# Gated mix of full and dilated local attention on one core: result products of two score sets together, bounds as sign-masked query rows, two head groups in the same rows

## The chip, the cores and the metric

The kernel runs on one core of a Trainium2 chip. The metric is the device time of one execution in microseconds (us). The kernel before has a median of 978.01 us over three runs (965.67, 978.01 and 978.8 us). The profile is of one execution, whose span from the first to the last instruction is 971.8 us.

## The reference

The input x is 2048 rows of 512 bf16 values. Two attention blocks with 32 heads of 16 values each run on the same x and are mixed by a gate per row:

```python
g = sigmoid((x * gate_w).sum(-1, keepdims=True))
# A: full attention
scores = einsum("bhqd,bhkd->bhqk", q, k) * (Dh ** -0.5)
a = (softmax(scores) @ v) @ A_wo
# B: 8 keys per row, at distances 0, 2, ..., 14; rows before the first are masked
b = (local dilated attention of x with B_wqkv) @ B_wo
out = g * a + (1 - g) * b
```

Here q, k and v are x @ wqkv, cut into heads. B_x isn't used.

## The kernel before, in words

**Block A.** The queries come in 4 chunks of 512 and the heads in 8 groups of 4. One chunk and one group make a *period*; there are 32. In a period, the unit of work is a *block*: one head's scores of 128 keys against 512 queries, 64 blocks to a period. PE makes the scores (q_proj and k_proj give `qt` and `kt_all`; each head fills 32 rows, 16 of values, one of a bound and 15 of zeros), four heads in four row groups of the array. ScalarE takes the exponential out of PSUM into a bf16 tile `pT`. PE multiplies that by the values `vp_all`, whose 17th column is 1 and so gives the softmax's denominator, into the one PSUM bank `acc`, four heads in four column groups.

Blocks go through PSUM in *sets* of alternately 3 and 2 (rings rA and rB, one buffer each); one activation covers a set. `pT` has two buffers per ring. The exponential needs no exact row maximum: a bound on each score is subtracted, sum of |q| times the largest |k|. For that, q_proj writes qt with a shift of 175 in the bound row, takes the absolute values (`absq`), multiplies them on PE by `selk_all` (minus the largest |k| in a column for the bound row) and adds the product to qt.

**VectorE blocks.** The last blocks of a period (`n_dve` of them, 129 in all) have their exponential made by VectorE in place of ScalarE, from a score in PSUM tag `misc`: step `dt` (linear, fp32), two steps `dg` and one `pd`, which build the bf16 bits. The three steps after dt take two blocks at once if there are two. Their values are scaled by 2^-56 in `vd_all`, a copy of the last two key tiles of vp_all.

**End of a period.** VectorE transposes acc in 32x32 squares (`accT`), divides by the denominator (`rden`, `ott`), and transposes back into `oat`. A head group of 4 heads fills 64 of the 128 rows of one slice of oat, eight slices per chunk, and the output product uses `woarr`, whose unused rows are zero.

**Block B** goes in 16 tiles of 128 rows, spaced 46.7 us in the plan. PE projects, VectorE evicts (`kvs`, `qb`), SP stores keys and values to DRAM and loads them back shifted (`ksh`, `vsh`). GpSimd multiplies and adds (`prod`, logits `lg`), VectorE and ScalarE do the small softmax (`mx`, `lg`, `ssum`, `rr`), GpSimd applies it to the values (`ob`, `obb`), PE transposes (`obt`).

**Order.** Each step is an Op with an engine, a duration in the planner's mind, what it needs, the buffers that it takes, and a due time. list_schedule (line 76) makes of them one fixed order per engine, in which each engine then runs (chain_on, line 180). An engine that waits for one step holds up all behind it. Where the result products of the last 3.2 us of the plan are few, the planner adds a *filler* in front of a result product: four matmuls that add zeros to acc (`acc<-ones_t,z`, line 789 on), to keep PE busy.

**Lines that matter here.** mm_heads 215, init 286 to 308, loads 318 to 356, k_proj 399, selk 423, v_proj 442, q_proj 482, b_tile 573, result products pv_mm 744 and the set loop 760 to 805, VectorE blocks d_group 809, end of a period 874 to 900, output products 906 to 980. In the profile, all operations of VectorE, ScalarE, GpSimd and SP that go through the chain have line 200, all matmuls line 209; the tiles tell them apart.

Of the kernel before, what the change touches and what calls it, by code (L numbers as in the profile page):

```python
# [18 lines left out]
    n_dve=(2,) * 4 + (3,) * 4 + (4,) * 17 + (6,) * 6 + (5,),  # L19
    dve_tiles=2,  # L20
    b_start=32.0,
# [13 lines left out]
SHIFT = 175.0  # L35
DEXP = 56
FRAC = 65536.0
# [18 lines left out]
class Op:  # L56

    def __init__(self, eng, occ, fn, dl, deps=(), alloc=(), use=(), lat=None, rel=0.0, name="",
                 dense=0, fill=False, after=()):
        self.eng, self.occ, self.fn, self.dl, self.rel, self.name = eng, occ, fn, dl, rel, name  # L60
        self.dense, self.fill, self.filled = dense, fill, False
        self.after = [d for d in after if d is not None]
        self.deps, self.alloc = [d for d in deps if d is not None], list(alloc)
        self.lat = (occ if not callable(occ) else occ(0.0)) + LAT[eng] if lat is None else lat
        self.done = None
        for tk in list(alloc) + list(use):
            tk.ops.append(self)
# [4 lines left out]
WAVE = lambda n: 0.2 + 0.22 * n  # L72
# [3 lines left out]
def list_schedule(ops):  # L76
# [28 lines left out]
    out, recent = [], []  # L105
    while len(out) < len(ops):
# [15 lines left out]
        lat = o.lat  # L122
        if o.dense:
# [19 lines left out]
def kernel(  # L143
# [71 lines left out]
    def mm_heads(out, c, col, rhs, start, stop):  # L215
        for j in range(4):
            mm(out[32 * j:32 * j + 32, :], wst[:, c, col + j * DH:col + j * DH + 32], rhs, start, stop, tile_position=(0, 32 * j))
# [16 lines left out]
    UNIT = 0.457  # L234
    T0 = 22.0
# [23 lines left out]
    wst = const.tile([128, DC, 3 * D], BF16, name="wst")  # L259
# [6 lines left out]
    woarr = const.tile([128, NG, D], BF16, name="woarr")  # L266
# [3 lines left out]
    rowc = const.tile([128, 3], FP32, name="rowc")  # L270
    z32 = const.tile([128, 32], BF16, name="z32")
    selq = const.tile([128, 128], BF16, name="selq")
# [3 lines left out]
    vd_all = const.tile([128, NTD, H, DH + 1], BF16, name="vd_all")  # L276
    kmax_all = const.tile([128, NG, NC], FP32, name="kmax_all")
    kmax = const.tile([128, NG], FP32, name="kmax")
    selk_all = const.tile([128, NG, 128], BF16, name="selk_all")
# [6 lines left out]
    def init_dve():  # L286
        V.memset(ones_t[:], 1.0)
        V.memset(selq[:], 0.0)
        V.memset(rowc[:], 0.0)
        for j in range(4):  # L290
            V.memset(selq[32 * j:32 * j + DH, 32 * j + DH:32 * j + DH + 1], 1.0)
            V.memset(rowc[32 * j:32 * j + DH + 1, 1:2], 1.0)
            V.memset(rowc[32 * j:32 * j + DH + 1, 2:3], SHIFT)
            V.memset(rowc[32 * j:32 * j + DH, 0:1], 1.0)
            V.memset(rowc[32 * j:32 * j + DH, 1:3], 0.0)
# [6 lines left out]
    def init_pool2():  # L302
        make_identity(nc, identf[:])
        G.memset(vp_all[:, 0, :, :], 1.0)
        G.memset(vp_all[:, 1:NT, :, DH:DH + 1], 1.0)

    def init_pool3():
        G.memset(woarr[:], 0.0)
# [4 lines left out]
    o_wz = op("pool", 3.6, init_pool3, -7.0, deps=[o_init_p])  # L313
# [4 lines left out]
    def load_x(sc):  # L318
        def s():
            if sc < 2:  # L320
                xl = work.tile([128, W, D], BF16, name="xld", tag="ksh", bufs=2)
            else:
                xl = work.tile([128, NG, QW], BF16, name="xld2", tag="oat", bufs=2)
# [3 lines left out]

    def load_w(part):
        def s():
            SP.dma_start(out=wst[:, :, part * D:(part + 1) * D], in_=a_w3[:, :, part * D:(part + 1) * D])  # L330
# [7 lines left out]
    def load_wo():  # L338
        SP.dma_start(out=bwo[:], in_=B_wo.rearrange("(c p) n -> p c n", p=128))
        wo4 = A_wo.rearrange("(i j d) n -> j d i n", j=4, d=DH)  # L340
        for j in range(4):
            SP.dma_start(out=woarr[32 * j:32 * j + DH, :, :], in_=wo4[j])
        SP.dma_start(out=kv_scr[0:16, 0:D], in_=woarr[16:32, 0, :])
        SP.dma_start(out=kv_scr[0:16, D:2 * D], in_=woarr[16:32, 1, :])
# [4 lines left out]
    o_wk = op("sp", 0.5, load_w(1), -8.9, lat=6.5)  # L349
    o_x[1] = op("sp", 0.5, load_x(1), -8.8, alloc=[xtok[1]], lat=7.5)  # L350
    o_x[2] = op("sp", 0.5, load_x(2), -8.7, alloc=[xtok[2]], lat=9.5)
    o_wq = op("sp", 0.5, load_w(0), -8.6, lat=11.0)
    o_x[3] = op("sp", 0.5, load_x(3), -8.5, alloc=[xtok[3]], lat=12.0)
    o_wv = op("sp", 0.5, load_w(2), -8.4, lat=13.0)
    o_bw = op("sp", 1.0, load_bw, -8.3, lat=19.0)
    o_wo = op("sp", 3.5, load_wo, -8.2, deps=[o_wz], lat=24.0)


    def warm():
        t_ = misc_ps([128, QW])  # L360
        for _ in range(3):
            mm_ct(t_, selq[:], ones_t[:], True, True)
# [36 lines left out]
    def k_proj(i, sc, tag, dl, rel=0.0):  # L399
# [3 lines left out]
        def part(c0, c1):  # L403
            def s():
                if c0 == 0:
                    st["pk"] = misc_ps([128, QW], tag=tag)
                for c in range(c0, c1):
                    mm_heads(st["pk"], c, D + 4 * i * DH, xT[:, c, sc * QW:(sc + 1) * QW], c == 0, c == DC - 1)
# [6 lines left out]
        def km():  # L415
            V.tensor_reduce(out=kmax_all[:, i, sc:sc + 1], in_=kt_all[:, i, sc * QW:(sc + 1) * QW],
                            axis=AX.X, op=ALU.max, apply_absolute_value=True)
        a = op("pe", WAVE(2), part(0, 2), dl - 2.6, dense=8, deps=[o_wk, o_init_d] + o_xt[sc], alloc=[tk], rel=rel, name=f"kp{i}.{sc}")
        b = op("pe", WAVE(2), part(2, DC), dl - 2.0, dense=8, deps=[a], use=[tk])
        c = op("dve", 0.71, kc, dl - 0.8, deps=[b], use=[tk])  # L420
        return op("dve", 0.70, km, dl, deps=[c])

    def selk(i, dl):
        def s():
            V.tensor_reduce(out=kmax[:, i:i + 1], in_=kmax_all[:, i, :], axis=AX.X, op=ALU.max)
            V.tensor_scalar(out=selk_all[:, i, :], in0=selq[:], scalar1=kmax[:, i:i + 1], scalar2=-1.0,
                            op0=ALU.mult, op1=ALU.mult)
        o_selk[i] = op("dve", 0.55, s, dl, deps=o_kc[i])
# [13 lines left out]
    def v_proj(h0, h1, tb, TB, tag, dl, rel=0.0):  # L442
# [4 lines left out]
        def mk(half):  # L447
            def s():
                if half == 0:
                    st["pv"] = misc_ps([128, TB, n], tag=tag)  # L450
                for tt in range(half * TB // 2, (half + 1) * TB // 2):
                    t = tb + tt
                    for c in range(DC):
                        mm(st["pv"][:, tt, :], xT[:, c, t * 128:(t + 1) * 128],
                           wst[:, c, 2 * D + h0 * DH:2 * D + h1 * DH], c == 0, c == DC - 1)
            return s

        def ev():
            V.tensor_copy(out=vp_all[:, tb:tb + TB, h0:h1, 0:DH], in_=st["pv"][:].rearrange("p t (h d) -> p t h d", d=DH))
            for t in range(max(tb, NT - NTD), tb + TB):  # L460
                V.tensor_scalar(out=vd_all[:, t - (NT - NTD), h0:h1, :], in0=vp_all[:, t, h0:h1, :],
                                scalar1=2.0 ** -DEXP, scalar2=None, op0=ALU.mult)
        xs = [o for sc in range(NC) if sc * TPC < tb + TB and (sc + 1) * TPC > tb for o in o_xt[sc]]
        a = op("pe", 0.62, mk(0), dl - 2.0, dense=8, deps=[o_wv] + xs, alloc=[tk], rel=rel, name=f"vp{h0}.{tb}")
        b = op("pe", 0.62, mk(1), dl - 1.4, dense=8, deps=[a], use=[tk])
        c = op("dve", 0.72 + 0.27 * max(0, tb + TB - (NT - NTD)), ev, dl, deps=[b, o_init_p], use=[tk])
# [15 lines left out]
    def q_proj(pi, tag, dl, rel=0.0):  # L482
# [4 lines left out]
        ta = tok("absq", 1)  # L487
        q_tok[pi] = tq

        def part(c0, c1):  # L490
            def s():
                if c0 == 0:
                    st["p1"] = misc_ps([128, QW], tag=tag)
                    st["absq"] = work.tile([128, QW], BF16, name="absq", tag="absq", bufs=1)
                    qt_tiles[pi] = work.tile([128, QW], BF16, name="qt", tag="qt", bufs=3)
                for c in range(c0, c1):
                    mm_heads(st["p1"], c, 4 * i * DH, xT[:, c, c_ * QW:(c_ + 1) * QW], c == 0, c == DC - 1)
            return s

        def ab():  # L500
            V.tensor_scalar(out=qt_tiles[pi][:], in0=st["p1"][:], scalar1=rowc[:, 0:1], scalar2=rowc[:, 2:3],
                            op0=ALU.mult, op1=ALU.add)
            V.tensor_scalar(out=st["absq"][:].bitcast(U16), in0=qt_tiles[pi][:].bitcast(U16), scalar1=32767,
                            scalar2=None, op0=ALU.bitwise_and)

        def bd():
            mm_ct(st["p1"], selk_all[:, i, :], st["absq"][:], True, True)

        def ev():
            V.tensor_tensor(out=qt_tiles[pi][:], in0=qt_tiles[pi][:], in1=st["p1"][:], op=ALU.add)  # L510
        a = op("pe", WAVE(2), part(0, 2), dl - 4.0, dense=8, deps=[o_wq, o_init_d] + o_xt[c_] + ([o_selk[i]] if pi else [o_kc[0][1]]), alloc=[tk, ta, tq], rel=rel, after=[last_q[0]], name=f"qp{pi}")
        last_q[0] = a
        b = op("pe", WAVE(2), part(2, DC), dl - 3.4, dense=8, deps=[a], use=[tk])
        c = op("dve", 1.25, ab, dl - 2.6, deps=[b], use=[tk, ta, tq])
        d = op("pe", WAVE(1), bd, dl - 1.4, dense=4, deps=[c, o_selk[i]], use=[tk, ta])
        o_q[pi] = op("dve", 0.71, ev, dl, deps=[d], use=[tk, tq])
# [56 lines left out]
    def b_tile(t):  # L573
# [153 lines left out]
        a = op("pe", 0.5, fin, tb + 62, dense=8, deps=[a1] + o_obt[-1:], alloc=[tk] + ([obt_tok[cb]] if tl == 0 else []), use=[tbb] + ([obt_tok[cb]] if tl else []))  # L727
# [31 lines left out]
    ex_ops, last_qk = [], [None]  # L759
    for k, us in enumerate(sets):  # L760
# [5 lines left out]
        tp = tok("pT" + ring, 2)  # L766
# [9 lines left out]
        def ex(us=us, st=st, ring=ring, maxn=maxn, n=n):  # L776
            st["p"] = work.tile([128, maxn, QW], BF16, name="pT", tag="pT" + ring, bufs=2)
            A.activation(out=st["p"][:, 0:n, :], in_=st["r"][:, 0:n, :], func=ACT.Exp, scale=float(DH) ** -0.5)
        kd = [o_kc[periods[pi][1]][t // TPC] for pi, t, j in us]
        a = op("pe", 0.30 + 0.02 * n, qk, tn - 3.0, deps=[o_q[pi] for pi in pis] + kd,  # L780
               alloc=[tr_], use=[q_tok[pi] for pi in pis], lat=0.52, after=[last_qk[0]], name=f"qk{k}")
        last_qk[0] = a
        b = op("act", 0.455 * n, ex, tn, deps=[a], alloc=[tp], use=[tr_], name=f"ex{k}")
        ex_ops.append(b)
        for pi in pis:
            mine = [(s_, t, j) for s_, (p_, t, j) in enumerate(us) if p_ == pi]

            def pv(pi=pi, mine=mine, st=st):
                if st["op", pi].filled:
# [3 lines left out]
                for s_, t, j in mine:  # L793
                    pv_mm(pi, t, j, st["p"][:, s_, :], vp_all[:, t])
            first = pi not in o_first
            o = op("pe", 0.21, pv, tn + 2.2, dense=len(mine), fill=not first, deps=[b] + [o_v[(4 * periods[pi][1] + j, t)] for _, t, j in mine]
                   + ([] if first else [o_first[pi]]),
                   alloc=[acc_tok[pi]] if first else [], use=[tp] + ([] if first else [acc_tok[pi]]), name=f"pv{k}")
            st["op", pi] = o
# [3 lines left out]
            if t_first[pi] < 4:  # L803
                t_first[pi] += sum(1 for _, t, j in mine if t == 0)
# [212 lines left out]
```

## Time and profile before

| What | Value |
|---|---|
| median of three runs | 978.01 us |
| span of the profiled execution | 971.8 us |
| ScalarE busy | 889.1 us (91%) |
| PE busy (matmuls, as modelled) | 846.7 us (87%) |
| VectorE busy | 733.9 us (76%) |
| GpSimd busy | 726.8 us (75%) |
| mean granted PE clock | 0.957 |
| first exponential of a set starts | 27.1 us |
| last one ends | 963.2 us |

A row of a group gives line, engine, operation, output tile<-input tiles, shapes and count, then the busy time, the mean length of one, and the idle time of the engine in front of it with what ended it. A row of the timeline gives start, length, engine, operation, count, and in brackets the idle time before. A row of stages gives the stretch, its length, then busy time and count for PE, PEld (weight loads), DVE (VectorE), ACT (ScalarE) and POOL (GpSimd), then the granted clock of PE, the share of the DMA engines and GB/s. ScalarE's busy share is that of a bound. PE's is lengthened by the tails of the matmuls.

### The profile page before, as it was taken

How to read it: one execution, taken by the hardware profiler on the slowest of the kernel's cores; microseconds unless marked ns; L12 is line 12 of the kernel's file. 1: busy time of each engine (PE TensorE's matmuls, PEld its weight loads, DVE VectorE, ACT ScalarE, POOL GpSimd, SP SyncE). 2: the span in 40 equal slices, each digit the busy share in tenths (PEclk: the TensorE clock that was granted, in tenths of full speed). 3: DMA queues.
4: the chain of work that ended last, by engine and by line, in shares of the span. 5: the costliest groups of instructions: out<-in, count | busy, mean ns of one | idle time of the engine just before them, and what ended most of it. 6: DMA issues, size and time to landing. Idle time of an engine off the chain costs nothing.

```text
span 971.8 us, 20318 instructions
## 1 busy us (share of the span) xinstructions
PE 846.7 (87%) x8495; PEld 270.0 (28%) x8495; DVE 733.9 (76%) x892; ACT 889.1 (91%) x790; POOL 726.8 (75%) x540
## 2 busy tenths in 40 slices
PE   7998999898989888988899988988899986898896
PEld 4333333232222322222233222222222221222221
DVE  5488788788667889887975887767885698876755
ACT  2898999898999999999999999899999977899986
POOL 2087969596999599999999999999999199900000
PEclk9999999999899999999999999798989989899998
DMA  9301111111030302020211021202110201000000
GB/s 261 100 3 55 45 56 45 55 45 55 1 104 12 103 1 99 11 88 13 86 61 51 12 98 36 64 1 98 55 45 12 96 14 45 2 1 1 1 2 22
DMA packets 43940, 47.49 MB, mean 49 GB/s; under 512 B 1812, under 2 KB 41284, under 8 KB 43848
## 3 DMA queue, kind: packets, MB, share of 16 engines
q1 hardware_dynamic: 43848, 46.19, 14.8%
q8 instruction: 66, 1.08, 0.4%
q14 instruction: 26, 0.21, 0.1%
HBM read 39.86 MB, written 6.33 MB: 48 GB/s over the span
## 4 chain that ended last, share of the span: by engine, by line
ACT 34%; PE 23%; DVE 21%; issue 16%; POOL 4%; DMA 1%; ACTq 0%; SPq 0%; DVEq 0%; POOLq 0%
ACT pT L200 33%; DVE dg L200 9%; PE acc L209 8%; PE ring L209 7%; PE misc_ps L209 6%; DVE pd L200 4%; POOL prod L200 4%; DVE dt L200 2%; PE misc L209 1%; DVE lg L200 1%; DVE qt L200 1%; DMA xld<-in_A_x_dram 1%; DVE accT L200 1%; DVE absq L200 1%; DVE rr L200 1%
## 5 line engine op out<-in xcount | busy, mean ns | idle before, releaser
L200 ACT ACTIVATE pT<-ring 128x1536 bf16<-128x1536 f32 (+2 forms) x768 | 881.2, 1292 | 60.2 <-PE ring L209 38.3
L209 PE MATMUL ring<-qt,kt_all 32*128 32x512 bf16 x1919 | 311.0, 393 | 83.5 <-ACT pT L200 77.3
L209 PE MATMUL acc<-pT,vp_all 128*17 128x512 bf16 (+1 forms) x1919 | 307.2, 398 | 6.5 <-DVE accT L200 4.6
L200 POOL TENSOR_TENSOR prod<-prod 128x512 f32<-128x512 f32 (+1 forms) x208 | 303.0, 1469 | 6.3
L200 POOL TENSOR_TENSOR prod<-ksh,qb 128x512 f32<-128x512 bf16 x128 | 183.5, 1464 | 61.9 <-DMA ksh<-kv_scr 59.5
L209 PEld LDWEIGHTS <-kt_all 32*128 32x128 bf16 x2048 | 110.1, 91 | 400.5 <-issue 394.4
L200 POOL TENSOR_TENSOR prod<-vsh,lg 128x512 f32<-128x512 bf16 x128 | 164.4, 1315 | 50.0 <-issue 25.0
L200 DVE TENSOR_SCALAR dt<-misc 128x512 f32<-128x512 f32 x129 | 88.5, 686 | 77.7 <-PE misc L209 70.0
L209 PE MATMUL acc<-ones_t,z 128*32 128x512 bf16 x1042 | 123.4, 412 | 0.0
L200 DVE SCALAR_TENSOR_TENSOR dg<-dt,dg 128x1024 bf16<-128x1024 uint16 (+1 forms) x67 | 118.4, 1767 | 1.6
L200 DVE SCALAR_TENSOR_TENSOR pd<-dg,dt 128x1024 uint16<-128x1024 bf16 (+1 forms) x67 | 113.7, 1697 | 1.8
L200 DVE SCALAR_TENSOR_TENSOR dg<-dt 128x1024 bf16<-128x1024 uint16 (+1 forms) x67 | 101.8, 1520 | 1.8
L209 PEld LDWEIGHTS <-vp_all 128*17 128x17 bf16 (+1 forms) x1919 | 71.7, 90 | 106.1 <-issue 99.9
L209 PE MATMUL misc_ps<-xT,wst 128*32 128x512 bf16 x1024 | 92.0, 393 | 0.2 <-DVE qb L200 0.2
L209 PE MATMUL misc_ps<-bw,xT 128*32 128x512 bf16 x768 | 70.0, 387 | 0.4 <-DVE vp_all L200 0.2
L209 PE MATMUL misc<-qt,kt_all 32*128 32x512 bf16 x129 | 50.7, 393 | 0.0
L209 PE MATMUL misc_ps<-woarr,oat 128*32 128x512 bf16 x512 | 46.1, 395 | 2.3 <-DVE oat L200 2.3
L209 PEld LDWEIGHTS <-z 128*32 128x32 bf16 x1042 | 29.6, 94 | 65.0 <-issue 64.5
L209 PE MATMUL acc<-pd,vd_all 128*17 128x512 bf16 x129 | 30.1, 404 | 14.4 <-DVE pd L200 14.4
L209 PEld LDWEIGHTS <-xT 128*32 128x32 bf16 (+1 forms) x1088 | 34.6, 96 | 27.2 <-issue 17.9
L200 DVE TENSOR_TENSOR qt<-qt,misc_ps 128x512 bf16<-128x512 bf16 x32 | 21.8, 682 | 24.4 <-PE misc_ps L209 24.2
L200 DVE TENSOR_SCALAR kt_all<-misc_ps,rowc 128x512 bf16<-128x512 f32 x32 | 25.7, 803 | 17.1 <-PE misc_ps L209 17.1
(71 smaller groups left out, 529.0 us busy)
## 6 DMA issues: line engine op xcount, KB each, us to landing
ksh<-kv_scr SPq DMA_DIRECT2D x16, 1024.0 KB, 5.6
vsh<-kv_scr SPq DMA_DIRECT2D x16, 1024.0 KB, 6.2
kv_scr<-kvs SPq DMA_DIRECT2D x16, 256.0 KB, 2.0
xld<-in_A_x_dram SPq DMA_DIRECT2D x4, 512.0 KB, 6.1
out_dram<-osb SPq DMA_DIRECT2D x16, 128.0 KB, 1.7
wst<-in_A_wqkv_dram SPq DMA_DIRECT2D x3, 512.0 KB, 9.0
bw<-in_B_wqkv_dram SPq DMA_DIRECT2D x1, 1536.0 KB, 11.6
bwo<-in_B_wo_dram SPq DMA_DIRECT2D x1, 512.0 KB
```

What stands on the lines that cost most here:

```text
L200: return chain_on(key, f(*a, **k))
L209: return chain(nc.tensor.matmul(out, lhsT=lhsT, rhs=rhs, start=start, stop=stop, **kw))
```

## The change

- *Result products together.* The result products of a set of 3 and the following set of 2 are one Op of five matmuls in place of two Ops; at most one filler then stands in front of five. pT has three buffers per ring.
- *Bounds.* The weights for q and k are written twice (`wtw`, 16 columns and the same 16 again), by eight copies of VectorE from `wraw`. So q stands in rows 0 to 15 and again in 16 to 31 of a head. Rows 16 to 31 are multiplied by the largest |k| of that row (`rowq`, with the eviction of qt) and get the sign bit set (`signm`, a bitwise or); the rows of kt_all beside them hold 1. The product with absq and the add to qt are gone. kmax comes from PSUM.
- *Shift and scale.* The shift is now the exponential's bias, an operand read from a tile (`lift`, 43.75 + 56 ln 2); before, it was the constant 0. All values are scaled by 2^-56, so vd_all is gone.
- *Two head groups.* The results of an even and an odd period stand in the same slice of `ott`, rows 0 to 15 and 16 to 31 of each head; one transpose to oat for both, four slices per chunk, output weights `wop` loaded by eight DMAs (woarr: four, and a memset by GpSimd).
- *VectorE blocks.* n_dve is 5 in place of 4 for periods 8 to 24 and 5 in place of 6 in period 25: 145 blocks in all. A period of 5 has two groups of two and one single.
- The planner's durations for PE are smaller, and it adds 0.13 us where PE changes between score products and others.

Counts in the instruction order of the two kernels: fillers 1042 to 660, matmuls 8495 to 7729, exponentials 768 to 761.

```diff
-    n_dve=(2,) * 4 + (3,) * 4 + (4,) * 17 + (6,) * 6 + (5,),
+    n_dve=(2,) * 4 + (3,) * 4 + (5,) * 18 + (6,) * 5 + (5,),
     dve_tiles=2,
+    p_bufs=3,
...
-SHIFT = 175.0
 DEXP = 56
+SHIFT = 43.75
+LIFT = SHIFT + DEXP * LN2
...
-WAVE = lambda n: 0.2 + 0.22 * n
+WAVE = lambda n: 0.03 + 0.205 * n
+TURN = 0.13
...
+        if e == "pe":
+            if o.rows != rows:
+                occ, lat = occ + TURN, lat + TURN
+            rows = o.rows
...
-            mm(out[32 * j:32 * j + 32, :], wst[:, c, col + j * DH:col + j * DH + 32], rhs, start, stop, tile_position=(0, 32 * j))
+            mm(out[32 * j:32 * j + 32, :], wtw[:, c, part, 4 * i + j, :, :].rearrange("p r d -> p (r d)"), rhs, start, stop,
+               tile_position=(0, 32 * j))
...
+    def twice(part, h0, h1):
+        def s():
+            for r in range(2):
+                V.tensor_copy(out=wtw[:, :, part, h0:h1, r, :],
+                              in_=wraw["t"][:, part * DC:(part + 1) * DC, h0 * DH:h1 * DH].rearrange("p c (h d) -> p c h d", d=DH))
         return s
...
+            for g in range(2):
+                SP.dma_start(out=wop[32 * j + DH * g:32 * j + DH * (g + 1), :, :], in_=wo4[j, g])
...
-            V.tensor_reduce(out=kmax_all[:, i, sc:sc + 1], in_=kt_all[:, i, sc * QW:(sc + 1) * QW],
-                            axis=AX.X, op=ALU.max, apply_absolute_value=True)
+            V.tensor_reduce(out=kmax_all[:, i, sc:sc + 1], in_=st["pk"][:], axis=AX.X, op=ALU.max,
+                            apply_absolute_value=True)
...
-            V.tensor_scalar(out=selk_all[:, i, :], in0=selq[:], scalar1=kmax[:, i:i + 1], scalar2=-1.0,
-                            op0=ALU.mult, op1=ALU.mult)
+            V.scalar_tensor_tensor(out=rowq[:, i:i + 1], in0=kmax[:, i:i + 1], scalar=rowc[:, 1:2], in1=rowc[:, 0:1],
+                                   op0=ALU.mult, op1=ALU.add)
...
-        def ab():
-            V.tensor_scalar(out=qt_tiles[pi][:], in0=st["p1"][:], scalar1=rowc[:, 0:1], scalar2=rowc[:, 2:3],
-                            op0=ALU.mult, op1=ALU.add)
-            V.tensor_scalar(out=st["absq"][:].bitcast(U16), in0=qt_tiles[pi][:].bitcast(U16), scalar1=32767,
-                            scalar2=None, op0=ALU.bitwise_and)
-
-        def bd():
-            mm_ct(st["p1"], selk_all[:, i, :], st["absq"][:], True, True)
 
         def ev():
-            V.tensor_tensor(out=qt_tiles[pi][:], in0=qt_tiles[pi][:], in1=st["p1"][:], op=ALU.add)
+            V.tensor_scalar(out=qt_tiles[pi][:], in0=st["p1"][:], scalar1=rowq[:, i:i + 1], scalar2=None, op0=ALU.mult)
+
+        def sg():
+            qb_ = qt_tiles[pi][:].bitcast(U16)
+            V.tensor_scalar(out=qb_, in0=qb_, scalar1=signm[:, 0:1], scalar2=None, op0=ALU.bitwise_or)
...
-            st["p"] = work.tile([128, maxn, QW], BF16, name="pT", tag="pT" + ring, bufs=2)
-            A.activation(out=st["p"][:, 0:n, :], in_=st["r"][:, 0:n, :], func=ACT.Exp, scale=float(DH) ** -0.5)
+            st["p"] = work.tile([128, maxn, QW], BF16, name="pT", tag="pT" + ring, bufs=cfg["p_bufs"])
+            A.activation(out=st["p"][:, 0:n, :], in_=st["r"][:, 0:n, :], func=ACT.Exp, scale=float(DH) ** -0.5, bias=lift[:, 0:1])
...
+        pend.append((us, st, tp, b))
+        if len(pend) < 2 and k + 1 < len(sets):
+            continue
+        members, pend = pend, []
+        for pi in sorted(set(u_[0] for m_ in members for u_ in m_[0])):
+            mine = [(st_, s_, t, j) for us_, st_, tp_, b_ in members for s_, (p_, t, j) in enumerate(us_) if p_ == pi]
...
+                for st_, s_, t, j in mine:
+                    pv_mm(pi, t, j, st_["p"][:, s_, :], vp_all[:, t])
...
-                pv_mm(pi, t, j, st["pd"][:, q_, :], vd_all[:, t - (NT - NTD)])
+                pv_mm(pi, t, j, st["pd"][:, q_, :], vp_all[:, t])
...
-            V.tensor_tensor(out=ott2[:, pi % 2, :, 0:DH], in0=st["a"][:, :, 0:DH], in1=rd_bc, op=ALU.mult)
+            g0 = DH * (pi % 2)
+            V.tensor_tensor(out=ott2[:, pi // 2 % 2, :, g0:g0 + DH], in0=st["a"][:, :, 0:DH], in1=rd_bc, op=ALU.mult)
...
-                    mm_ct(st["pf"], oat_tiles[c_][:, k, tt * 128:(tt + 1) * 128], woarr[:, k, :], k == 0, k == ng - 1)
+                    mm_ct(st["pf"], oat_tiles[c_][:, k, tt * 128:(tt + 1) * 128], wop[:, k, :], k == 0, k == ng - 1)
```

## Prediction

> **What bounds the kernel now.** I read the page's engine shares first, then ScalarE's groups, then its timeline, then three stages, then the waits.
>
> ```profile
> span 971.8 us, 20318 instructions
> ...
> PE 846.7 (87%) x8495; PEld 270.0 (28%) x8495; DVE 733.9 (76%) x892; ACT 889.1 (91%) x790; POOL 726.8 (75%) x540
> ...
> L200 ACT ACTIVATE pT<-ring 128x1536 bf16<-128x1536 f32 (+2 forms) x768 | 881.2, 1292 | 60.2 <-PE ring L209 38.3
> ```
>
> ScalarE's exponentials are the bound: 881.2 us of them, with 60.2 us of idle in front. The timeline of ScalarE gives its undisturbed step and the start:
>
> ```profile
> 27.10 13.79 ACT L200 ACTIVATE pT<-ring 128x1536 bf16<-128x1536 f32 x12 [8.40 <-PE ring L209]
> ...
> 726.53 27.23 ACT L200 ACTIVATE pT<-ring 128x1536 bf16<-128x1536 f32 x24 [0.50 <-PE ring L209]
> ```
>
> 24 exponentials are 12 pairs of 3+2 blocks, 60 blocks in 27.2 us: 0.452 us a block. One activation lasts 1504 ns (by form), of which 1536 elements at 0.833 ns leave 224 ns of fixed part; the next one starts after 1331 ns in unbroken runs of the timeline, so all but about 51 ns of that part is hidden under the one before.
>
> Stages, cut at the accT transposes that end periods 7 and 27 (timeline of VectorE), and at the last exponential:
>
> ```profile
> 27.10:272.70 245.60, 222.10 (x2384) 76.55 (x2383) 188.55 (x256) 229.53 (x205) 186.72 (x146) 0.98 0.15 50
> 272.70:854.70 582.00, 506.87 (x4914) 153.50 (x4914) 452.42 (x498) 550.82 (x490) 533.19 (x384) 0.95 0.15 48
> 854.70:963.20 108.50, 95.91 (x923) 28.70 (x923) 73.22 (x88) 103.46 (x92) 0.00 (x0) 0.97 0.00 1
> ```
>
> Columns: length, then PE, PEld, DVE, ACT, POOL busy, clock. With 492, 1194 and 233 blocks at 0.452 us, and 4+12 small lg exponentials at 0.42 us, ScalarE alone would need 224.1, 544.7 and 105.3 us. The excess is 21.5 (A), 37.3 (B) and 3.2 us (C), 62.0 together; 27.1 us of start and 8.6 us of end complete the 971.8. Of the 62.0, 51.8 us (60.2 less the 8.4 at the start) is ScalarE idle, and PE ends most of it:
>
> ```profile
> ACT pT L200 <- PE ring L209: 38.3, 43, 8.4
> ...
> DVE qt L200 <- PE misc_ps L209: 27.3, 22, 3.5
> ...
> ACT pT L200 <- PE acc L209: 18.7, 17, 5.3
> PE acc L209 <- DVE pd L200: 14.4, 14, 2.1
> ```
>
> The last line is how a late VectorE reaches ScalarE: PE stands in order before the products of pd, and the next score products stand behind them.
>
> **The change part by part.** The sum is against this execution (971.8 us span); the median of the three runs is 978.01, 1.0064 times that, and I scale at the end.
>
> *PE.* One pair of sets now:
>
> ```profile
> 896.60 0.39 PE L209 MATMUL ring<-qt,kt_all 32*128 32x512 bf16 x3 [0.64 <-ACT pT L200]
> 896.92 0.40 PE L209 MATMUL acc<-ones_t,z 128*32 128x512 bf16 x4
> 897.15 0.39 PE L209 MATMUL acc<-pT,vp_all 128*17 128x512 bf16 x3
> 897.52 0.39 PE L209 MATMUL ring<-qt,kt_all 32*128 32x512 bf16 x2
> ```
>
> Start to start: 0.23 us for a group of four in the same direction, 0.32 to 0.37 where the next group is of the other kind, so about 0.1 us per turn. By the instruction order of both kernels the runs of one kind go from 1550 to 1186: 364 x 0.1 = 36 us of turns; 382 fewer fillers are 95 groups x 0.23 = 22 us; 256 fewer output products 64 x 0.22 = 14 us; 128 fewer bound products 7 us. 79 us of PE go, but they count only where ScalarE waits for PE.
>
> *ScalarE.* 16 blocks fewer: 16 x 0.452 = 7.2 us. Each of the 761 exponentials now reads its bias from a tile; before it was the constant 0. No row shows that on ScalarE. From below: 0, hidden like the rest of the fixed part. From above, the nearest rows: VectorE's fa<-misc_ps,g_sp with one such operand takes 745 ns, dt<-misc without 686 ns, so 59 ns, 44.9 us in all. I take 14 ns, since 51 of 224 ns of the fixed part are not hidden (23% of 59): 10.6 us. The Trainium skill, page "ScalarE: Activation LUTs", section "What ACT_TABLE_LOAD costs", speaks against the change here: it says that a pointer operand adds about 93 ns to an activation. Unhidden, that would be 70.8 us; no run here shows it yet.
>
> *VectorE.* In stage B 86 blocks become 102. A period of 5 is two pairs and a single. From the groups by form at 100 to 750 us: a pair's three steps 1661+1930+1865 = 5.456 us, a single's 1154+1594+1192 = 3.940, dt 0.685. 43 pairs become 42 pairs and 18 singles: -5.5 +70.9; 16 more dt: +11.0; 20 final adds on qt go (0.682, the sign step costs what absq did): -13.6; 10 oat transposes go (0.709): -7.1. Load: 452.4 + 55.8 = 508.2 us. Two stretches that VectorE filled before:
>
> ```profile
> 791.50:825.80 34.30, 25.77 (x230) 7.30 (x228) 30.58 (x32) 27.15 (x24) 33.22 (x23) 0.90 0.12 36
> 825.80:854.70 28.90, 24.38 (x217) 6.70 (x217) 26.28 (x28) 25.47 (x22) 23.99 (x15) 0.88 0.01 1
> ```
>
> Even there it idles 3.7 and 2.6 us a period. Some of these waits go with the bound product (27.3 us of waits over 32 periods) and the turns, so I take 2.6: 508.2 + 20 x 2.6 = 560.2 us. ScalarE's own line in B is 1178 x 0.452 + 5.0 + 471 x 0.014 = 544.1. So VectorE becomes the bound of B, at 560.2 against 582.0: -21.8. The outer values are 544.1 and, with 3.9 us (with a third full stretch, 5.3 us at 207.7), 586.
>
> *Stage A.* VectorE loses 16 us there (8 qt adds 5.4, 4 oat 2.8, vd_all 4.1, selk_all 8 x 0.5) and PE its share of the 79. I take 12 of the 21.5 us of excess as left, plus 197 x 0.014: -6.7 (bounds +2.8, all excess stays, and -18.7).
>
> *Start.* The doubled weights are eight copies by VectorE before the first scores: 256 elements about 0.25 us, 1792 about 1.0 us (xT's 1024-element copy takes 0.69), 5 us, part of it under waits for DMA; selk_all, absq, the bound product and the add leave (some 2 us). I take +2.0, between -2 and +5. On SP eight wop loads stand where four woarr stood (four took 2.77 us to issue), before the first ksh load; GpSimd waited for that until 46.2 us anyway, and no longer behind two z_scr stores (4.5 us). Third pT buffers, vp_all's scaling and kmax from PSUM cost nothing: same instructions, the same 0.68 us.
>
> *End and C.* Same blocks in C; 93 x 0.014 = 1.3 us, and 0.8 for a later GpSimd: +2.1.
>
> Sum: 971.8 + 2.0 - 6.7 - 21.8 + 2.1 = 947.4 us, times 1.0064 = 953.
>
> **Rivals.** (1) *VectorE's waits stay*: B takes 586, the span 973.2, time 979. For it: the 3.9 us of the full stretches. Against: two of PE's three reasons to be late shrink.
> (2) *GpSimd paces B.* obb takes 1266 to 2136 ns by its tile view, and VectorE's pair steps, which take about 1.22 us after 875 us where GpSimd is done, take up to 1.93 beside it: each slows the other. At the shortest durations of each kind a tile of GpSimd needs 36.4 us; it takes 719.9/16 = 45.0. The 8.6 us lost, over some 18.2 us of such VectorE steps a tile (292 us outside C, by the groups), are 0.47 us per us, and there are 65.5 us more: +31. If GpSimd's 84 us of idle between 46 and 851 stays, its last logits come at 839 instead of 813, and 258 blocks follow: span 988. If half goes, 946, hidden. Midpoint 967, time 973.
> (3) *The bias read is paid in full* (the other side): 59 ns x 761. ScalarE's line is 27.1 + 860.2 + 6.7 + 8.6 = 902.6, +2 start, +44.9, +36 excess (VectorE is then no bound, and some idle stays) = 985.5, time 992, slower than before. It decides from about 41 ns on, where the sum reaches 971.8. For it: the fixed part is visible in each activation; against: 173 of 224 ns are hidden now. By the Trainium skill's 93 ns the span would be 1011 and the time 1018.
> (4) *The clock gate.* The granted clock halves after stretches in which PE did little:
>
> ```profile
> 611.20:614.60 3.40, 1.94 (x22) 0.66 (x15) 3.37 (x5) 3.40 (x4) 3.40 (x3) 1.00 0.41 120
> 614.60:618.00 3.40, 3.22 (x20) 0.60 (x19) 3.15 (x7) 3.38 (x4) 3.24 (x3) 0.50 0.55 189
> ...
> 884.20:887.60 3.40, 2.36 (x27) 0.77 (x25) 3.10 (x4) 3.40 (x4) 0.00 (x0) 1.00 0.00 0
> ```
>
> 1.94 us of 3.4 was followed by half speed, 2.36 not. The pair of the changed order (score products of both sets, filler, five result products) is 0.39 us, then 0.32 + 0.23 + 0.22 + 0.39 = 1.16: busy 1.55 in 2.26 us, 2.34 in 3.4, the edge. Now 8.6% of the time is at half speed (mean clock 0.957, twice what is missing), some 25 of 285 such stretches. If 100 more were, each would cost 0.44 us (five groups of twice 0.22 and 0.4 of turns, 2.6 us a pair against 2.26, 1.5 pairs) to 0.84 (ScalarE's idle in two such stretches, 0.02 and 1.65): +64, span 1011, time 1018. The Trainium skill, page "TensorE: Matmul & The Clock Gate", section "Why this matters for your kernels", asks only that PE have no idle gaps over about 3 us; by that the clock and the sum would stay, but the 1.94 us row shows a drop without such a gap.
> (5) *VectorE fits in*: ScalarE's line 902.6 + 2 + 10.6, with 20 us of excess: 935, time 941; 930 with a free bias.
>
> **How the numbers follow.** Forecast 0.38 (own range 944 to 962), (1) 0.14, (2) 0.08, (3) 0.12, (4) 0.06, (5) 0.22. 2%, about what a measurement of this kernel can tell from no change, is 958 to 998. Faster: 0.28 of the forecast and all of (5), 0.50. Slower: (4) and 0.05 of (3), 0.11. Same: 0.39. Range 930 to 992: below it 0.06, above it (4) and half of (3), 0.12.
>
> **What would show it.** Unbroken runs of pT at 1.34/0.92 us a step confirm the bias price (1.39/0.96 would be rival 3); first exponential at 29; VectorE over 88% busy in B with PE acc waiting for pd more than 14.4 us, and B at 560; granted clock near 0.95; GpSimd's last obb by 865. I am wrong if VectorE's waits do not shrink or the bias read shows in full.

## The result, and the profile after

The changed kernel takes **1035.69 us** (median of four runs, 1034.51 to 1038.2), against 975.52 us for the kernel before (four runs by now): 1.0634 times as long, 95% interval 1.057 to 1.070. It is slower, and outside the predicted range. The profiled execution spans 1036.4 us, 64.6 more than the 971.8 of before. Medians here take in every execution and ratios only undisturbed ones; of e3 below, the profiled execution was a disturbed one of 1644 us, so e3 has times and no trace. From the page:

```profile
span 1036.4 us, 18777 instructions
...
PE 875.5 (84%) x7729; PEld 252.9 (24%) x7729; DVE 749.5 (72%) x903; ACT 950.4 (92%) x783; POOL 726.9 (70%) x539
...
PEclk9999999999898886876789998766577898688786
...
L209 ACT ACTIVATE pT<-ring,lift 128x1536 bf16<-128x1536 f32 x761 | 942.8, 1376 | 64.0 <-PE ring L218 58.8
...
L218 PE MATMUL acc<-ones_t,z 128*32 128x512 bf16 x660 | 90.4, 488 | 0.0
```

Seven exponentials fewer take 61.6 us more in all, and the clock row (tenths of full speed, 40 slices) falls to 5 and 6 in places. PE issues 766 matmuls fewer and is busy 29 us longer: the same groups take longer at half speed. ScalarE's timeline, two unbroken runs:

```profile
27.66 14.72 ACT L209 ACTIVATE pT<-ring,lift 128x1536 bf16<-128x1536 f32 x12 [8.83 <-PE ring L218]
...
201.81 29.51 ACT L209 ACTIVATE pT<-ring,lift 128x1536 bf16<-128x1536 f32 x24 [1.12 <-PE ring L218]
```

24 exponentials took 27.23 us before and take 29.51: 95 ns more each. In the trace, the median distance from start to start where they follow without a gap goes from 1331 to 1423 ns (three blocks) and from 904 to 996 ns (two). That is 92 ns in both shapes, so it is a price per instruction: 761 x 92.5 = 70.4 us.

The same three stages (periods 0 to 7, 8 to 27, the rest), columns as before:

```profile
27.66:282.10 254.44, 219.74 (x2292) 77.40 (x2291) 179.26 (x238) 245.05 (x204) 181.05 (x141) 0.96 0.16 51
282.10:909.10 627.00, 532.57 (x4375) 138.64 (x4372) 473.43 (x526) 587.86 (x485) 530.94 (x382) 0.80 0.14 44
909.10:1027.90 118.80, 102.26 (x796) 26.04 (x796) 75.06 (x86) 112.14 (x91) 11.47 (x8) 0.77 0.00 1
```

A is 8.8 us longer, B 45.0, C 10.3. VectorE is busy for 76% of B and PE waits for its results (pd) for 7.2 us in the whole run, so it isn't the bound there. The waits:

```profile
ACT pT L209 <- PE ring L218: 58.8, 88, 8.8
...
PE acc L218 <- DVE pd L209: 7.2, 13, 1.3
```

ScalarE's 18.7 us of waiting for acc are gone. PE's wait for pd is half of what it was, but that comes with the slower exponentials, as e1 and e4 below show. And waiting for ring costs 58.8 us instead of 38.3. Laid beside the granted clock, ScalarE's idle time between the first and the last exponential (52.1 us before, 55.1 now) has moved. Idle stretches that touch half clock, or the 3 us behind it, made 29.5 us and now make 52.3; the others made 22.6 and now make 2.8. (Counting only the time inside half clock, 23.2 became 46.5.) Time at half clock after 25 us went from 86 to 335 us. How a drop comes about (stages of 3.4 us around 717 us):

```profile
710.30:713.70 3.40, 3.22 (x34) 0.80 (x26) 2.35 (x3) 3.40 (x4) 3.01 (x3) 1.00 0.67 223
713.70:717.10 3.40, 1.78 (x15) 0.58 (x15) 3.29 (x5) 3.40 (x4) 0.00 (x0) 1.00 1.10 364
717.10:720.50 3.40, 2.83 (x19) 0.59 (x15) 2.50 (x4) 3.14 (x3) 0.73 (x1) 0.50 0.12 36
...
734.20:737.60 3.40, 3.40 (x21) 0.62 (x20) 0.52 (x2) 3.13 (x4) 3.40 (x4) 0.50 0.02 5
```

PE was busy for 1.78 of 3.40 us, in 15 matmuls; then the clock is 0.50 for seven stretches. The timeline of PE inside the second row:

```profile
714.41 0.39 PE L218 MATMUL ring<-qt,kt_all 32*128 32x512 bf16 x3 [0.51 <-ACT pT L209]
714.74 0.40 PE L218 MATMUL acc<-ones_t,z 128*32 128x512 bf16 x3
714.96 0.39 PE L218 MATMUL acc<-pT,vp_all 128*17 128x512 bf16 x3
715.42 0.39 PE L218 MATMUL ring<-qt,kt_all 32*128 32x512 bf16 x2
716.85 0.44 PE L218 MATMUL ring<-qt,kt_all 32*128 32x512 bf16 x3 [1.04 <-ACT pT L209]
```

With the result products of two sets due together, nothing stands between the score products of 715.42 and 716.85, and PE waits 1.04 us for ScalarE. The drop needs no long gap.

### The profile page after: what moved, and what is told of

Read it like the earlier page. It is cut to its first block, busy times and chain, and to the rows that moved or that the text cites. A ratio compares the mean times of both kernels' runs of the same rounds, so it can differ in the third digit from the quotient of the medians.

```text
span 1036.4 us, 18777 instructions
## 1 busy us (share of the span) xinstructions
PE 875.5 (84%) x7729; PEld 252.9 (24%) x7729; DVE 749.5 (72%) x903; ACT 950.4 (92%) x783; POOL 726.9 (70%) x539
## 4 chain that ended last, share of the span: by engine, by line
ACT 36%; PE 30%; issue 23%; DVE 9%; DMA 1%; SPq 0%; DVEq 0%; ACTq 0%
ACT pT L209 35%; PE acc L218 12%; PE ring L218 10%; PE misc_ps L218 6%; DVE dg L209 3%; DVE pd L209 2%; PE misc L218 2%; DVE dt L209 1%; DMA z_scr<-zrow 1%; DMA xld<-in_A_x_dram 1%; PE misc_ps L736 1%; ACT lg L209 1%; PE pxt L401 0%; DVE accT L209 0%; DVE kt_all L209 0%
## 5 line engine op out<-in xcount | busy, mean ns | idle before, releaser
L209 ACT ACTIVATE pT<-ring,lift 128x1536 bf16<-128x1536 f32 x761 | 942.8, 1376 | 64.0 <-PE ring L218 58.8
L218 PE MATMUL ring<-qt,kt_all 32*128 32x512 bf16 x1903 | 342.1, 440 | 136.9 <-ACT pT L209 127.1
L218 PE MATMUL acc<-pT,vp_all 128*17 128x512 bf16 (+1 forms) x1903 | 281.3, 449 | 0.3 <-DVE accT L209 0.3
L209 DVE SCALAR_TENSOR_TENSOR pd<-dg,dt 128x1024 uint16<-128x1024 bf16 (+1 forms) x84 | 134.2, 1598 | 2.4
L209 DVE SCALAR_TENSOR_TENSOR dg<-dt,dg 128x1024 bf16<-128x1024 uint16 (+1 forms) x84 | 134.2, 1597 | 2.0
L218 PE MATMUL misc_ps<-xT,wtw 128*32 128x512 bf16 x1024 | 93.8, 423 | 1.6 <-DVE kmax_all L209 1.5
L218 PE MATMUL acc<-ones_t,z 128*32 128x512 bf16 x660 | 90.4, 488 | 0.0
L218 PE MATMUL acc<-pd,vp_all 128*17 128x512 bf16 x145 | 42.8, 470 | 7.2 <-DVE pd L209 7.2
L209 DVE STREAM_TRANSPOSE accT<-acc 128x512 f32<-128x512 f32 x32 | 22.8, 712 | 34.3 <-PE acc L218 34.2
L218 PEld LDWEIGHTS <-wtw 128*32 128x32 bf16 x1024 | 23.9, 99 | 38.7 <-issue 26.7
```

The costliest lines, as they stand in the source:

```text
L209: return chain_on(key, f(*a, **k))
L218: return chain(nc.tensor.matmul(out, lhsT=lhsT, rhs=rhs, start=start, stop=stop, **kw))
```

## The experiments

Theory A: the exponential's bias read from `lift`. Theory B: the clock, through the fillers that the pairing lost. Rival: VectorE with 145 blocks. "Waiting" is ScalarE's idle time between first and last exponential in the profiled run, "half" the part of it in idle stretches that touch half clock or the 3 us behind it. Ratios are to the kernel before, run on the same chip, with a median of 976.92 us beside e1 to e4, 971.96 beside e5 to e8 and 977.32 beside e9 to e12.

| Run | median us | ratio, 95% interval | clock | fillers | waiting, half |
|---|---|---|---|---|---|
| before | 975.52 | 1 | 0.957 | 1042 | 52.1, 29.5 |
| changed | 1035.69 | 1.063 (1.057-1.070) | 0.839 | 660 | 55.1, 52.3 |
| e1 no pointer | 982.58 | 1.007 (1.003-1.011) | 0.894 | 660 | 61.0, 50.7 |
| e2 two fillers | 1001.64 | 1.030 (1.021-1.038) | 0.970 | 1800 | 27.6, 16.7 |
| e3 both | 967.69 | 0.994 (0.991-0.998) | - | 1800 | - |
| e4 before + pointer | 1027.3 | 1.057 (1.045-1.068) | 0.952 | 1042 | 35.0, 16.4 |
| e5 row, two fillers | 969.34 | 0.999 (0.995-1.003) | 0.967 | 1800 | 54.8, 21.6 |
| e6 same, 129 blocks | 951.16 | 0.980 (0.974-0.987) | 0.987 | 1829 | 29.2, 10.0 |
| e7 unpaired | 995.0 | 1.026 (1.020-1.033) | 0.977 | 1356 | 17.1, 8.1 |
| e8 row, unpaired | 958.43 | 0.987 (0.981-0.993) | 0.970 | 1356 | 41.0, 20.4 |
| e9 unpaired, few fillers | 1034.56 | 1.057 (1.050-1.065) | 0.862 | 611 | 51.8, 44.7 |
| e10 row, unpaired, 129 | **945.04** | **0.967 (0.962-0.972)** | 0.967 | 1305 | 27.6, 19.5 |
| e11 e10, more fillers | 960.55 | 0.983 (0.977-0.989) | 0.971 | 1776 | 42.1, 17.9 |
| e12 e10, two buffers | 946.62 | 0.969 (0.963-0.975) | 0.974 | 1380 | 31.8, 12.8 |

**e1, the pointer.** `bias=lift[:, 0:1]` is dropped from the activation; the kernel so leaves out the shift of ScalarE's blocks.

> The changed kernel with the exponential's bias given as an immediate zero in place of the pointer to lift; the factor e^82.6 of ScalarE's blocks is left out, all else is as changed. Theory A (the pointer): each of the 761 exponentials pays 92 to 93 ns (steps of 1.423 and 0.996 us against 1.331 and 0.903), so the steps fall back to 1.331 and 0.903 and some 70 us go, less what new waits for TensorE take back: 966 if the 55 us of ScalarE's waiting stay as they are, up to 985 if the lower clock now holds it up more. Theory B (the clock gate paces, the pointer only fills waiting that would be there anyway): the steps get shorter by 0.093 but the waiting grows by nearly as much, 1010 to 1036, at a clock no higher than 0.839.

```profile
L209 ACT ACTIVATE pT<-ring 128x1536 bf16<-128x1536 f32 x761 | 877.2, 1285 | 67.7 <-PE ring L218 62.2
...
PE acc L218 <- DVE pd L209: 20.8, 27, 1.9
```

Steps are back at 1330 and 903 ns; 53 us go, to a time that theory A expected (966 to 985). ScalarE's exponentials alone are 65.6 us shorter (942.8 to 877.2), and its waiting grows by 6. Theory A holds for most of the loss, but not for all: without the pointer the changed kernel is still no faster than the kernel before, at a clock of 0.894. PE now waits 20.8 us for pd, more than the 14.4 of the kernel before: the 7.2 us of the changed kernel hold only beside its slow ScalarE.

**e4, the pointer alone**, on the kernel before, to a tile of zeros (`bias=zb[:, 0:1]`).

> The kernel before with its exponentials reading their bias from a pointer to a tile of zeros; the values are the same. Theory A: 768 x 92.5 ns = 71 us, less what of its 52 us of waiting the longer steps absorb: steps of 1.423 and 0.996, time 1010 to 1046. Theory B (the pointer costs little by itself, the price in the changed kernel comes from the slow clock): within 10 us of the kernel before, 970 to 985.

```profile
L200 ACT ACTIVATE pT<-ring,zb 128x1536 bf16<-128x1536 f32 (+2 forms) x768 | 945.8, 1393 | 42.9 <-PE ring L209 27.6
```

881.2 us of exponentials become 945.8, and this edit alone brings the kernel before to 1.057, where the whole change stands at 1.063. Of the 71 us, 17 vanish in waiting that shrinks from 52.1 to 35.0; PE's wait for pd falls to 9.6 us by the pointer alone.

**e2, more fillers**, pointer kept; DENSE_MIN is 28 in place of 20 and MAXF is 2. The main lines of the edit:

```diff
...
-            if o.fill and sum(x[1] for x in recent) + n < DENSE_MIN:
-                o.filled = True
+            while o.fill and o.filled < MAXF and sum(x[1] for x in recent) + n < DENSE_MIN:
+                o.filled += 1
...
```

> The changed kernel with up to two filler groups ahead of a paired result operation while fewer than 28 matmuls stand in the window: 1800 fillers for 660, the pointer stays. Theory B (the clock gate is what lost the time): the clock comes back to 0.95 or more, the 52 us of ScalarE's waiting in half-clock windows go, and the time falls to 975 to 990. Theory A (the pointer is most of it): the steps stay at 1.423 and 0.996, so no less than 920.6 of steps + 27 ahead + 9 behind = 980 can come out; with 10 to 30 us of waiting left, 985 to 1010. If the fillers themselves are now too much for TensorE: no gain, 1030 or more at a high clock.

```profile
PEclk9999999999899989999999999999899998989998
...
L218 PE MATMUL acc<-ones_t,z 128*32 128x512 bf16 x1800 | 166.3, 400 | 0.0
```

The clock is back at 0.970 and 34 us go; ScalarE's waiting in half-clock stretches falls from 52.3 to 16.7 us, while the steps stay at 1423 and 997. PE does 1140 matmuls more and is busy 38 us less (837.3 us). The clock is as theory B expected; the time is in theory A's 985 to 1010, since the pointer's price stays.

**e7 and e9, the pairing.** e7 issues the result products after each set again (`len(pend) < 1`); e9 does too, with DENSE_MIN 14.

> The changed kernel with the result products issued after each set again, all else as changed, the pointer too: 1356 fillers come out of the unchanged filler rule for 660. If the pairing is what took the clock: clock 0.94 or more, waiting in half-clock windows below 25 us, time 1000 to 1020. If the pairing has no part in it: 1030 to 1042 at 0.84.

> The changed kernel, pointer and 145 blocks, with result products after each set and the filler rule's minimum lowered from 20 to 14 matmuls: 611 fillers, near the 660 of the pairing, but spread over the sets. If the number of fillers is what keeps the clock: clock 0.82 to 0.88 and 1020 to 1040, as with the pairing. If the spacing is (two sets' products in one burst, then a gap): clock 0.93 or more and 990 to 1005.

The page of e9:

```profile
PEclk9999899999898898767579988679968898888986
...
L218 PE MATMUL acc<-ones_t,z 128*32 128x512 bf16 x611 | 82.5, 478 | 0.0
```

Unpaired, the same rule places 1356 fillers and the time falls by 41 us (36 by the ratios), to 5 us below the range expected of e7; with about as few fillers as the pairing leaves, it is 1034.56 us again. So the pairing loses the clock mainly through the number of fillers. Its bursts can account for little: with 611 fillers and no pairing the clock is 0.862, with 660 and pairing 0.839. And ScalarE does not wait for acc in e7 either: that gain did not need the pairing.

**e3, both.**

> Immediate bias and the two fillers together. If the pointer (70 us) and the waiting at half clock (52 us) are separate losses that add: 1036 - 70 - 30 to 50 = 915 to 935, faster than the kernel before. If the one hides in the other: 950 to 975. If VectorE or GpSimd then becomes the bound: 940 to 960 with waits for acc and pd in the chain.

e1's and e2's edits together take 967.69 us. Apart they took off 53 and 34 us, together 68: the two losses don't add to 915-935, and something else holds the kernel.

**e5 and e6, a bias-free kernel that computes the reference.** The lift goes into the score product: row 16 of each head holds 330 instead of its part of the bound. Both have e2's fillers. The step that puts it in (the constants that it reads are changed with it):

```diff
...
-            V.tensor_scalar(out=qt_tiles[pi][:], in0=st["p1"][:], scalar1=rowq[:, i:i + 1], scalar2=None, op0=ALU.mult)
+            V.tensor_scalar(out=qt_tiles[pi][:], in0=st["p1"][:], scalar1=rowq[:, i:i + 1], scalar2=lift[:, 0:1], op0=ALU.mult, op1=ALU.add)
...
```

> The lift moved out of the bias into the score product (one of the sixteen bound rows of a head holds the constant 330 and that dimension drops out of the bound), bias immediate, and two fillers as in the earlier run. Steps 1.331 and 0.903, so the time of the run that had both edits: 962 to 970. If VectorE is what holds it above the 915 to 935 that two separate losses gave, PE waits for pd for over 20 us in all and ScalarE's waiting falls outside the half-clock windows; if TensorE is (450 filler groups), ScalarE waits for ring products with VectorE's results long there.

> The same with the 129 VectorE blocks of the kernel before in place of 145: 768 exponentials, so 7 us more of ScalarE's steps and 16 blocks x 4.4 us = 70 us less of VectorE's work. If VectorE is now the bound: 935 to 955. If it is not: 968 to 978.

e5, the waits of PE:

```profile
PE ring L218 <- ACT pT L209: 75.6, 205, 1.5
PE acc L218 <- DVE pd L209: 31.7, 38, 2.5
```

31.7 us for pd, and 33 of ScalarE's 54.8 us of waiting at full clock. With 129 blocks (e6) that wait is 13.5 us and the time 18 us lower, 951.16, though ScalarE has 7 us more to do; that is in the 935 to 955 expected if VectorE was the bound. Part of the 18 us may be the clock, which goes from 0.967 to 0.987; e8 and e10 below repeat the step at an equal clock. So with the pointer gone the 145 blocks are a loss, which the changed kernel hides, as its ScalarE is slow. Whether VectorE itself or GpSimd beside it is late isn't separated: the chain of e5 runs 26% over GpSimd and 22% over VectorE.

**e8 and e10 to e12**, without pairing.

> Lift in the product, bias immediate, result products after each set again: what is left of the change is the bound rows, the two head groups, the third result buffer and the 145 blocks. If the clock and the pointer were all that was lost: faster than the kernel before, 940 to 960. If pairing was worth its 19 us of removed waits: 960 to 975, with those waits for pd back.

> Lift in the product, result products after each set, and 129 VectorE blocks for 145: 7 us more of steps on ScalarE, some 70 us less work for VectorE. If VectorE paces the run of 958 (PE waited 33 us for pd, chain 34% VectorE): 936 to 948. If it does not: 962 to 968.

> The last one with the filler minimum at 24 in place of 20: 1776 fillers for 1305. If half-clock windows still cost it: 5 to 12 us faster than that. If their time is gone already: the same within 4 us, or slower by up to 10 us where 118 more filler groups keep TensorE from the score products.

> Lift in the product, unpaired, 129 blocks, and two result buffers for three. If the third buffer is what took away ScalarE's waits for acc (18.7 us in the kernel before): 10 to 18 us slower than with three, with those waits back. If they went for another reason: the same within 4 us.

e8 takes 958.43 us, inside the 940 to 960 expected if clock and pointer were all that was lost. The page of e10, the fastest:

```profile
span 943.2 us, 20008 instructions
...
L209 ACT ACTIVATE pT<-ring 128x1536 bf16<-128x1536 f32 (+2 forms) x768 | 876.9, 1338 | 34.1 <-PE ring L218 30.5
```

e10 is 3.3% faster than the kernel before (interval 2.8 to 3.8). Of the change it keeps the bound rows, the shared output rows, the third buffer and the planner's new durations; it has no pointer, no pairing and no extra blocks. Which of the parts kept gives the 3.3% isn't separated, but for the buffer (e12). Against e8 the medians differ by 13 us (by the ratios, 2.0%) at a clock of 0.967 and 0.970: the 16 blocks again. e11 was a miss: 118 more filler groups cost 15 us at the same clock, since waiting at full clock rises from 8.1 to 24.2 us; the expectation allowed 10. e12 shows the third buffer to be worth nothing that can be told (0.969 against 0.967), with 8.7 us of ScalarE's waits for acc in place of 2.3. So the buffer removed at most a part of the 18.7 us of the kernel before, and what removed the rest isn't separated.

## Why the prediction was wrong

The sum was 947.4 us and the span is 1036.4: 89.0 too low. By its parts A is short by 15.5, B by 66.8 and C with the end by 8.2; the start was 1.4 too long (first exponential at 27.66, not 29; the copies of the weights took 3.0 us, not 5).

- **The bias price** is the step that failed: 14 ns taken, 92.5 measured. "51 of 224 ns of the fixed part are not hidden" supposed that a longer fixed part hides like the rest; the steps of 1.423 and 0.996 us show that none of the addition hides, beyond even the 1.39 and 0.96 that stood for rival (3). The upper bound was too low as well: 59 ns came from VectorE, another engine. The Trainium skill, page "ScalarE: Activation LUTs", section "What ACT_TABLE_LOAD costs", says that a pointer operand adds about 93 ns to an activation, and the trace agrees (92 ns in both shapes). With 92.5 in place of 14 the working gives A 254.4 us (measured 254.4) and C with the end +9.4 (measured +10.3): to within 1 us these two stages failed in this term alone, and the 12 us of excess taken for A came out.
- **VectorE as the bound of B** did not come in the changed kernel. With the true price ScalarE's own line in B is 544.1 - 6.6 + 43.6 = 581.1 us, above the 560.2 put down for VectorE. VectorE's load was 473.4 us, not 508.2: there its pair steps took 1529, 1764 and 1790 ns, not 1661, 1930 and 1865. That doesn't make the step right. In e5, which has neither the pointer's price nor the slow clock, B by the same cut (269.92 to 851.63 us) lasts 581.7 us: VectorE is busy for 505.7, near the 508.2 of the forecast, but idle for 76.0, or 3.8 us a period in place of 2.6. In e8 it is 3.1 (busy 513.1 of 575.9). So the 2.6 us were too few as well, which the other two losses hid. How much of e5's 3.8 its 1800 fillers cause is open.
- **The clock gate**, rival (4), came, with a chance of 0.06. B is 45.9 us longer than ScalarE's line (37.3 before). Of this, 39.1 us are ScalarE's idle time, all of it in stretches that touch half clock or the 3 us behind it (before, 22.0 of 31.2). The edge was placed well (1.94 to 2.36 us busy in 3.4; about 2.3 measured), yet the forecast kept the clock "near 0.95" (0.839 measured): the count of lost fillers (382 of 1042) was booked as a gain of 22 us for PE, and put at nothing as a cost. Its price: 249 us more at half clock are 73 stretches; e2 and e7 remove 272 and 287 us, 80 and 84 stretches, for 33 and 36 us by the ratios, 0.41 and 0.43 each, a little under the 0.44 to 0.84 given. The page "TensorE: Matmul & The Clock Gate" of the Trainium skill, section "Why this matters for your kernels", asks for no gap over some 3 us; the trace disagrees for this kernel: in the 3.41 us ahead of 39 of its 40 drops the longest pause of PE was 1.29 us or less, in the median 0.61.
- **Rival (3)**, the read in full, came too, at 1.6 times its price. Rivals (3) and (4) were priced singly, 992 and 1018, and given chances as if only one could be true. Together they overlap by only 17 us (e1 53 and e7 41 apart, e8 77 together). (1) can't be read from the changed kernel, whose slow ScalarE shortens the wait for pd; with pointer and clock mended in e5, B's 581.7 us are nearer its 586 than the forecast's 560.2, though e5 doesn't tell a late VectorE from a late GpSimd. (2) wasn't what held the changed kernel: GpSimd isn't in the chain of the changed kernel; its last obb starts at 919.5 us, not 865, as all else is later. (5), 941, is near e10's 945 by chance: e10 has neither pointer nor pairing nor 145 blocks.

## What to carry to other kernels

An operand that changes from a constant to a pointer in the bound engine's repeated instruction is a change to the bound itself: multiply its full price by the count, from start-to-start distances on that engine, and take no discount for what seems hidden. Work removed from PE is no gain while another engine is the bound, and can be a loss: count what PE has left to do in each 3.4 us. When a rival is not exclusive, price the two together.

## What the hardware showed

- A bias read from a tile costs ScalarE 92 to 93 ns per exponential, for 1024 and 1536 elements alike, unhidden in back-to-back runs; 50 us for this kernel before by the medians, 55 by the ratio (e4).
- PE's clock followed its busy time more closely than its pauses. Of the 3.41 us stretches at full clock, cut where the trace changes clock, 53 were followed by half clock in the two kernels, and 46 of these had PE busy (as modelled) below 2.3 us; of 395 that were not, 15 had. A pause of PE above 0.5 us sorts them less well: 51 of the 53 had one, but so had 88 of the 395.
- Doing more on PE made it less busy: 1140 matmuls of zeros more, 38 us less busy (e2). Past that the fillers stand in the way: 471 more cost 15 us at an unchanged clock (e11).
